# Moving the last score weights, the fold of q and the gate's small steps in a linear-attention and product-key kernel

## Chip, cores and metric

The kernel runs on one core of a Trainium2 chip. The metric is the device time of one launch in microseconds (us): the median of several runs. The profile is one further execution, taken by the hardware profiler. The engines are named as the profile names them: PE (TensorE; PEld is its weight load), DVE (VectorE), ACT (ScalarE), POOL (GpSimd) and SP (SyncE, which here only issues transfers).

## The reference, cut to what matters

One input x of 2048 rows and 512 columns goes through two branches, and a gate mixes them.

```python
g = sigmoid((x * gate_w).sum(-1, keepdims=True))
# branch A: linear attention, 32 heads of 16, feature map learned per head
q, k, v = x @ wqkv                       # split into heads
phi_q = concat(softmax(q @ w_phi), softmax(-(q @ w_phi)))
phi_k = concat(softmax(k @ w_phi), softmax(-(k @ w_phi)))
kv = sum_s phi_k[s]^T v[s];  z = sum_s phi_k[s]
a = (phi_q @ kv) / (phi_q @ z + 1e-6) @ wo
# branch B: product keys, 32 heads, 16 x 16 = 256 experts, the best one per head
s1 = (x @ w_q)[..., :128] @ k1.T;  s2 = (x @ w_q)[..., 128:] @ k2.T
e = 16 * argmax(s1) + argmax(s2)         # one expert per row and head
b = sum_h gelu(x . u[e_h]) * v[e_h]      # softmax over one score is 1
out = g * a + (1 - g) * b
```

## The kernel before

The 2048 rows are 16 tiles (`NT`) of 128. All large products are done in three passes on a value split into a rounded high half and the remaining low half (`xh`, `xl` and so on): high by high, high by low, low by high (`mm3`, lines 54 to 56). `split` makes the halves: ACT copies the high half, DVE subtracts.

The schedule is written by hand: each engine runs its instructions in the order in which the program issues them, and each waits for its data. So a waiting instruction holds everything behind it on its engine, and SP's transfers are in order too.

**First loop, t = 0 to 15 (line 283 on): the sums over k and the weights.** For each tile `vproj` and `kproj` project v and k on PE; `softmax_diffs` makes the differences for both softmaxes on DVE (lines 90, 92, 94, 96); ACT takes the exponential (L315); `ksoft` sums and inverts on DVE (L179, L180) and multiplies on POOL (L181); `kvacc` adds phi_k^T v on PE (L188). The last two tiles' sums are made after the loop, and `kvz` (L196) adds their z part with a column of ones.

Between these, the loop builds what the second loop needs. w_phi is folded into the weights of k and q (`fold`, PE L147, high halves ACT L137, low halves DVE L138; one pair of tiles, `wah` and `wal`, holds first k's and then q's folded weights). The product-key scores use w_q folded with the keys: for each of eight blocks j, `score_w` (L204) makes two products, `score_planes` copies the result as two 16-bit planes (ACT L209) and has the DMA transpose them (SP L211), and `score_join` puts the planes together (ACT L216), copies the high half into `sh` (ACT L220) and subtracts the low half into `sl` (POOL L221). The plane tile `wpl`, the transposed tile `wtp` and the joined tile `wtj` have one buffer each. `joins` holds blocks transposed but not joined; at the start of a tile's middle part they move to `old` and are joined at that tile's end, and in tile 15 ahead of its exponential. `plan` places the last products: block 6 is complete in tile 12, block 7 in tile 14. In tile 14, `eh` and `el`, the halves of the expert values, are split as well. In tile 15 PE folds q in two halves, with the two halves of the first tile's scores (`front_s`, s = x by `sh`/`sl`) behind them, and the fold is evicted after `ksoft`.

**Between the loops:** `kvz`, the best keys of tile 0 (`best`), the projection of q with the folded weights (`front_q`, tile pq), the gate and expert products (`front_p`, tile pp), the copy `zc` of the sums z, and `z_final`, which spreads z over all partitions on PE (L619).

**Second loop, a = 0 to 14, and a tail written out for the last tiles.** It is a software pipeline over three tiles: scores, q and gate of the next tile (n and a), the counting of chosen experts of tile b = a - 1 (`count`, a chain of some twenty small DVE steps that `step` deals out between others), and the output product of z = a - 2. `gelu_pre` and `gate` make the sigmoid of the gate from `exp(-p)`: `gs[:,0]` is the exponential, `gs[:,1]` adds one, `gs[:,2]` inverts, `gs[:,3]` is half of one minus the gate. `gelu_act` then applies the tanh and that factor. `coef` (L558) multiplies the counts by the activated values; it runs on POOL up to tile 13 and on DVE for 14 and 15.

Of the kernel before, what the change touches and what calls it, by code (L numbers as in the profile page):

```python
# [15 lines left out]
AF = mybir.ActivationFunctionType  # L16
ALU = mybir.AluOpType
# [6 lines left out]
NT = S // P  # L24
# [9 lines left out]
def mix_kernel(ctx, tc, xT, wqT, wkT, wv, wphi, wo, wq, kk, ug, ev, cst, out):  # L34
# [98 lines left out]
    def fold(raw, wh, wl, n_, halves=True):  # L133
        def evict(g):
            for q in range(4):
                part = o[q].rearrange("p (g c) -> p g c", c=32)[:, g]
                act.copy(fv(wh, q)[:, g], part)  # L137
                dve.tensor_tensor(fv(wl, q)[:, g], part, fv(wh, q)[:, g], op=ALU.subtract)  # L138

        o = [tr_bank(f"fold{n_}{q}") if q < 3 else mm_bank(f"fold{n_}{q}") for q in range(4)]  # L140
        for i in range(2):
            for k in (2 * i, 2 * i + 1):
                for b in range(NK):
                    for q in range(4):
                        r = slice(32 * q, 32 * q + 32)
                        c0 = (k * NK + b) * 32
                        pe.matmul(o[q][:, c0:c0 + 32], raw[r, b, k * P:(k + 1) * P], wp[r, b, :],  # L147
                                  start=True, stop=True, skip_group_check=True)
            yield
            if halves:  # L150
                evict(slice(8 * i, 8 * i + 8))
                yield
        if not halves:
            evict(slice(0, 16))
            yield
# [27 lines left out]
    def kvacc(t):  # L183
        n = F + 1 if t < NT - 2 else F
        for g in range(8):
            for c in range(4):
                h = 4 * g + c
                pe.matmul(acc[32 * c:32 * c + 32, g, :n], phis[t][:, 32 * h:32 * h + 32],  # L188
                          vs[t][:, h, :n], start=(t == 0 and g == 0),
                          stop=(t == NT - 1), skip_group_check=True)  # L190
# [23 lines left out]
    def score_join(j, tp):  # L214
        tj = wa_.tile([P, D], F32, tag="wtj", bufs=1, name=f"wtj{j}")
        act.copy(tj.bitcast(U16).rearrange("p (k n j) -> p j k n", j=2, n=P),  # L216
                 tp.rearrange("p (j k) n -> p j k n", j=2))
        js = slice(P * j, P * j + P)
        t3 = tj.rearrange("p (k e) -> p k e", k=NK)
        act.copy(sh[:, :, js], t3)  # L220
        pool.tensor_tensor(sl[:, :, js], t3, sh[:, :, js], op=ALU.subtract)  # L221
# [3 lines left out]
    def front_s(t, half):  # L225
        e = st8[t]
        e[half] = mm_bank(f"s{half}_{t}")
        proj(e[half], t, sh, sl, 512 * half, 512 * half + 512)
# [55 lines left out]
    for t in range(NT):  # L284
        if t + 3 < NT:
            x_load(t + 3)
        if 2 < t < NT - 2:
            vproj(t)()
        kproj(t)
        old = list(joins)  # L290
        joins.clear()
        for _ in range(plan.get(t, 0)):
            score_w(done, raws[done])
            done += 1
            if done + 1 < 16:
                raws.append(stage(wq[done + 1], f"wq{done + 1}"))
            elif done == 15:
                rawq = stage(wqT, "rawq")
            if done % 2 == 0:
                score_planes(done // 2 - 1)  # L300
        if t == 11:
            rawu = [spare(ug[:, 0:2], "rawu0", [P, 2, NU])]
        if t == 12:
            rawu.append(spare(ug[:, 2:4], "rawu1", [P, 2, NU]))
        if t == 13:
            rawe = [spare(ev[:, 0], "rawe0", [P, D])]
        if t % 2 == 0:
            for u in (t - 3, t - 2):
                if u >= 0:
                    kvacc(u)  # L310
        if t == NT - 1:
            for j, tp in old:
                score_join(j, tp)
            old = []
        act.activation(phis[t], phis[t], AF.Exp)  # L315
        if 0 < t < NT - 2:
            x_split(t + 2)
        if t == 13:
            for k in range(NK):
                split(uh[:, k, :], ul[:, k, :], rawu[k // 2][:, k % 2, :])  # L320
            rawe.append(spare(ev[:, 1], "rawe1", [P, D]))
        if t == 14:
            for k in range(2):
                split(eh[:, k, :], el[:, k, :], rawe[k])
        if t == NT - 1:
            fq = fold(rawq, wah, wal, "q", False)
            next(fq)
            front_s(0, 0)
            next(fq)
            front_s(0, 1)  # L330
            kvacc(NT - 3)
        ksoft(t)
        if t == NT - 1:
            next(fq)
        for j, tp in old:
            score_join(j, tp)
    ca.close()
# [19 lines left out]
    def gelu_pre(t):  # L357
        pp = st8[t]["pp"]
        gs = w2.tile([P, 4], F32, name=f"gs{t}", tag="gs")
        act.activation(gs[:, 0:1], pp[:, NX:NX + 1], AF.Exp, scale=-1.0)  # L360
        px = w2.tile([P, NX], F32, name=f"px{t}", tag="px")
        x2 = w2.tile([P, NX], F32, name=f"x2{t}", tag="x2")
        act.copy(px, pp[:, :NX])
        act.activation(x2, pp[:, :NX], AF.Square)
        act.activation(x2, x2, AF.Copy, bias=GELU_C, scale=0.044715 * GELU_C)
        st8[t].update(g=gs, G=px, x2=x2)

    def gate(t):
        gs = st8[t]["g"]
        yield dve.tensor_scalar_add(gs[:, 1:2], gs[:, 0:1], 1.0)  # L370
        yield dve.reciprocal(gs[:, 2:3], gs[:, 1:2])
        yield dve.tensor_scalar(gs[:, 3:4], gs[:, 2:3], -0.5, 0.5, op0=ALU.mult, op1=ALU.add)

    def gelu_in(t):
        px, x2 = st8[t]["G"], st8[t]["x2"]
# [1 line left out]

    def gelu_act(t):
        x2, gs = st8[t]["x2"], st8[t]["g"]
        act.activation(x2, x2, AF.Tanh)  # L380
        act.activation(x2, x2, AF.Identity, bias=gs[:, 3:4], scale=gs[:, 3:4])

# [9 lines left out]
    def soft_in(t, step=lambda: None):  # L392
        e = st8[t]
        d = w2.tile([P, 1024], F32, tag="d", name=f"d2{t}")
        st = w2.tile([P, 320], F32, tag="stt", name=f"st2{t}")
        softmax_diffs(e["pq"], d, st, step)
        e.update(ph=d, st=st)
# [157 lines left out]

    def coef(t):
        e = st8[t]
        (pool if t < NT - 2 else dve).tensor_tensor(e["C"], e["C"], e["G"], op=ALU.mult)  # L558

    def back_c(t):  # L560
        e = st8[t]
# [72 lines left out]
    turn_eq(0)  # L634
    front_q(0)
    soft_in(0)
    kvz(NT - 1)
    act.copy(zc, acc[:, :, F])
    front_p(0)
    z_final()  # L640
    wo_load((0, 1))
    for a in range(NT - 1):
        n, b, z = a + 1, a - 1, a - 2
        B, Z = b >= 0, z >= 0
        if Z:
            mid_num(z)
            back_c(z)
        if B:
            planes(b)
            front_q(a)  # L650
        if a == 1:
            v14, v15 = vproj(NT - 2), vproj(NT - 1)
        gelu_in(a)
        if Z:
            num_lo(z)
            back_cl(z)
        for _ in gate(a):
            step(b)
        gelu_act(a)
        if B:  # L660
            step(b, 2)
            soft_in(a, lambda: step(b, 2))
            drain(b)
        if a == 1:
            v14()
        soft_exp(a)
        if a == 1:
            v15()
            for k in range(2):
                act.copy(wbh[:, k, :], rawo[k])  # L670
        if Z:
            back_o(z)
            back_ol(z)
            back_out(z)
            store(z)
        mid_mask(a)
        front_s(n, 0)
        if a == 1:
            kvacc(NT - 2)
            kvacc(NT - 1)  # L680
            cl_.close()
            w4 = ctx.enter_context(tc_pool("w4", "right"))
        front_s(n, 1)
        front_p(n, False)
        soft_w(a)
        soft_sum(a, 0)
        soft_sum(a, 1)
        if a == 1:
            for k in range(2):
                pool.tensor_tensor(wbl[:, k, :], rawo[k], wbh[:, k, :], op=ALU.subtract)  # L690
            wo_load((2, 3))
        best(n, 0)
        soft_y(a, 0)
        soft_y(a, 1)
        if B:
            join(b)
            gelu_out(b)
            coef(b)
        if a == 1:
            kv_final()  # L700
            for k in range(2, NK):
                act.copy(wbh[:, k, :], rawo[k])
        soft_b(a)
        if a == 1:
            for k in range(2, NK):
                pool.tensor_tensor(wbl[:, k, :], rawo[k], wbh[:, k, :], op=ALU.subtract)
        best(n, 1)
        turn_eq(n)
        gelu_pre(n)
# [9 lines left out]
    for _ in gate(a):  # L719
        step(b)  # L720
    gelu_act(a)
    step(b, 2)
    soft_in(a, lambda: step(b, 2))
    drain(b)
    coef(b)
# [85 lines left out]
```

## Time and profile before

| | us |
|---|---|
| median of 3 runs (393.65 to 393.74) | 393.67 |
| the profiled execution | 393.26 |
| its span, from the first to the last instruction | 391.5 |
| mean granted clock of PE in it | 0.991 |

A row of the timeline gives the start, the duration, the engine, the line of the kernel, the operation, what it writes and reads, the shapes and how many instructions were put together; square brackets give how long the engine sat idle before it and for whom. Matmuls are pipelined: one of 512 columns is shown as some 0.4 us long, while the next starts about 0.23 us after it. In the waits, "A <- B: total, times, longest" says that A sat idle until B was done.

### The profile page before, as it was taken

The numbers are of one execution on the slowest core, as the hardware profiler recorded it, in microseconds if no ns is written. First come the engines' busy times: TensorE is split into PE (matmuls) and PEld (weight loads), VectorE is DVE, ScalarE is ACT, GpSimd is POOL, SyncE is SP. The second block draws the span as 40 slices with busy tenths as digits, with TensorE's granted clock in tenths as the row PEclk, the third lists the DMA queues.
The fourth block names the chain that finished last, engine by engine and source line by source line (L and its number), as shares of the span: only waits on it lengthen the run. The fifth ranks groups of instructions, "written<-read, shape, count | busy, mean of one in ns | idle before, by whom it ended". The sixth has DMA issues, their size and how long they took to land.

```text
span 391.5 us, 9209 instructions
## 1 busy us (share of the span) xinstructions
PE 381.0 (97%) x3688; PEld 297.9 (76%) x3688; DVE 324.1 (83%) x831; ACT 210.3 (54%) x358; POOL 155.1 (40%) x164
## 2 busy tenths in 40 slices
PE   8999999999999899999999999999999999999975
PEld 5866787777767688877878788788788788788753
DVE  4356866766668769989999999999999999999994
ACT  4325465644645344657557556555564574574732
POOL 1004344325324332756336346345344354264340
PEclk9999999999999899999999999999999999999989
DMA  7478867478692033130650430440431331323301
GB/s 280 150 265 295 208 251 229 155 211 243 209 268 68 4 82 80 55 83 29 108 82 27 109 81 28 103 87 28 86 84 47 82 82 56 80 57 80 83 27 55
DMA packets 66715, 45.38 MB, mean 116 GB/s; under 512 B 58096, under 2 KB 58992, under 8 KB 64368
## 3 DMA queue, kind: packets, MB, share of 16 engines
q1 hardware_dynamic: 65808, 43.92, 41.4%
q10 hardware_dynamic: 864, 0.87, 0.8%
q8 instruction: 29, 0.48, 0.5%
q14 instruction: 14, 0.11, 0.1%
HBM read 26.43 MB, written 4.19 MB: 78 GB/s over the span
## 4 chain that ended last, share of the span: by engine, by line
PE 78%; DVE 13%; ACT 4%; POOL 2%; issue 2%; DMA 1%; POOLq 0%; DVEq 0%; ACTq 0%
PE s L54 6%; PE s L55 6%; PE s L56 6%; PE pv L54 4%; PE po L579 4%; PE po L585 4%; PE po L580 3%; PE pv L56 3%; PE pv L55 3%; PE pq L54 3%; PE ws L204 3%; PE pq L56 3%; PE pq L55 3%; PE pk L56 3%; PE pk L55 3%; PE pk L54 3%
## 5 line engine op out<-in xcount | busy, mean ns | idle before, releaser
L410 POOL TENSOR_TENSOR w<-d,zb 128x512 f32<-128x512 f32 x32 | 40.8, 1297 | 100.8 <-ACT d L404 100.8
L181 POOL TENSOR_TENSOR d<-d,st 128x1024 f32<-128x1024 f32 x16 | 31.0, 1939 | 77.0 <-DVE st L180 70.5
L55 PE MATMUL s<-sl,xh 128*128 128x512 f32 x128 | 50.8, 397 | 2.1 <-POOL sl L221 2.1
L54 PE MATMUL s<-sh,xh 128*128 128x512 f32 x128 | 52.4, 409 | 0.0
L56 PE MATMUL s<-sh,xl 128*128 128x512 f32 x128 | 50.8, 397 | 0.0
L404 ACT ACTIVATE d<-d 128x512 f32<-128x512 f32 x32 | 18.4, 624 | 58.8 <-DVE d L96 58.8
L440 POOL TENSOR_TENSOR d<-d,st 128x512 f32<-128x512 f32 x31 | 32.7, 1075 | 25.9 <-DVE st L434 20.8
L483 ACT COPY pt<-tp 128x1024 uint16<-128x1024 uint16 x30 | 39.0, 1371 | 1.6 <-DMA tp<-pl 0.8
L315 ACT ACTIVATE d<-d 128x1024 f32<-128x1024 f32 x16 | 17.0, 1061 | 39.0 <-DVE d L96 39.0
L473 ACT COPY pl<-d 128x1024 uint16<-128x1024 uint16 x30 | 30.5, 1060 | 2.1 <-POOL d L440 2.0
L55 PEld LDWEIGHTS s<-sl,xh 128*128 128x128 f32 x128 | 24.4, 190 | 7.0 <-POOL sl L221 2.4
L129 DVE TENSOR_TENSOR xl<-xr,xh 128x512 fp32r<-128x512 f32 (+2 forms) x17 | 11.2, 661 | 21.4 <-ACT xh L128 21.3
L56 PEld LDWEIGHTS s<-sh,xl 128*128 128x128 f32 x128 | 24.5, 191 | 5.5
L54 PEld LDWEIGHTS s<-sh,xh 128*128 128x128 f32 x128 | 24.3, 190 | 4.7
L414 DVE TENSOR_REDUCE st<-d 128x32 f32<-128x512 f32 x32 | 20.5, 681 | 8.2 <-ACT d L404 8.2
L579 PE MATMUL po<-wbh,oh 128*128 128x512 f32 x64 | 26.0, 407 | 1.1 <-ACT oh L497 1.1
L54 PE MATMUL pv<-wbh,xh 128*128 128x512 f32 x64 | 26.6, 415 | 0.6 <-ACT xh L128 0.6
L54 PE MATMUL pq<-wah,xh 128*128 128x512 f32 x64 | 26.5, 415 | 0.0
L580 PE MATMUL po<-wbl,oh 128*128 128x512 f32 x64 | 25.9, 404 | 0.0
L56 PE MATMUL pv<-wbh,xl 128*128 128x512 f32 x64 | 25.4, 396 | 0.0
L54 PE MATMUL pk<-wah,xh 128*128 128x512 f32 x64 | 25.3, 396 | 0.0
L55 PE MATMUL pv<-wbl,xh 128*128 128x512 f32 x64 | 25.3, 395 | 0.0
(147 smaller groups left out, 1026.7 us busy)
## 6 DMA issues: line engine op xcount, KB each, us to landing
wq<-wq SPq DMA_DIRECT2D x16, 1024.0 KB, 6.2
xr<-xT SPq DMA_DIRECT2D x15, 256.0 KB, 5.6
y<-ot SPq DMA_DIRECT2D x15, 256.0 KB, 2.0
rawk<-wkT SPq DMA_DIRECT2D x1, 1024.0 KB, 6.0
rawq<-wqT SPq DMA_DIRECT2D x1, 1024.0 KB, 5.2
rawo<-wo SPq DMA_DIRECT2D x4, 256.0 KB, 3.6
rawu<-ug SPq DMA_DIRECT2D x2, 258.0 KB, 6.1
rawv<-wv ACTq DMA_DIRECT2D x2, 256.0 KB, 4.5
```

The costliest lines, as they stand in the source:

```text
L54: pe.matmul(o, ah, bh, start=(first and i == 0), stop=False)
L55: pe.matmul(o, ah, bl, start=False, stop=False)
L56: pe.matmul(o, al, bh, start=False, stop=(last and i == n - 1))
L181: pool.tensor_tensor(g64(d), g64(d), b64(st[:, 128:192]), op=ALU.mult)
L404: act.activation(d[:, s_], d[:, s_], AF.Exp)
L410: pool.tensor_tensor(e["w"][:, s_], e["ph"][:, s_], zb[:, s_], op=ALU.mult)
L414: dve.tensor_reduce(e["st"][:, 64 + 32 * i:96 + 32 * i], g64(e["ph"])[:, 32 * i:32 * i + 32], axis=AX.X, op=ALU.add)
L440: eng.tensor_tensor(g64(d)[:, gs_], g64(d)[:, gs_], r[:, gs_].unsqueeze(2).to_broadcast([P, 32, F]), op=ALU.mult)
L473: act.copy(pl, e["ph"][:, s_].bitcast(U16).rearrange("p (c j) -> p j c", j=2))
L483: act.copy(p16[:, :, 4 * i:4 * i + 4, :], e["tp"][i].rearrange("p (j g) n -> p j g n", j=2))
L579: pe.matmul(po, oh[:, k, :], wbh[:, k, :], start=(k == 0), stop=False)
L580: pe.matmul(po, oh[:, k, :], wbl[:, k, :], start=False, stop=False)
```

## The change

Five things are moved. (1) The join of block 6 goes from the end of tile 13 to tile 14, ahead of its exponential, and that of block 7 from tile 15 to tile 14, behind its exponential; so it now stands ahead of the split of `eh`/`el` on ACT and of `ksoft`'s product on POOL. (2) In tile 15 the fold of q, the first scores and `kvacc` of tile 13 are issued ahead of the exponential, and the fold's eviction with them, ahead of `ksoft`. (3) Between the loops `front_p(0)` is issued ahead of the last `kvz`. (4) Two of the three small DVE steps of the gate go to ACT, into `gelu_pre` and `gelu_act`; the number of `step` calls is made up behind it. (5) `coef` of tile 14 goes from DVE to POOL.

```diff
@@ first loop
-        old = list(joins)
-        joins.clear()
+        old = [] if t == NT - 3 else list(joins)
+        if old:
+            joins.clear()
...
-        if t == NT - 1:
-            for j, tp in old:
-                score_join(j, tp)
-            old = []
+        if t == NT - 2:
+            score_join(*old.pop())
+        elif t == NT - 1:
+            fq = fold(rawq, wah, wal, "q", False)
+            next(fq)
+            front_s(0, 0)
+            next(fq)
+            front_s(0, 1)
+            kvacc(NT - 3)
+            next(fq)
         act.activation(phis[t], phis[t], AF.Exp)
+        if t == NT - 2:
+            score_join(*joins.pop())
         if 0 < t < NT - 2:
             x_split(t + 2)
...
-        if t == NT - 1:
-            fq = fold(rawq, wah, wal, "q", False)
-            next(fq)
-            front_s(0, 0)
-            next(fq)
-            front_s(0, 1)
-            kvacc(NT - 3)
         ksoft(t)
-        if t == NT - 1:
-            next(fq)
         for j, tp in old:
             score_join(j, tp)
@@ gelu_pre, gate, gelu_act
         act.activation(gs[:, 0:1], pp[:, NX:NX + 1], AF.Exp, scale=-1.0)
+        act.activation(gs[:, 1:2], gs[:, 0:1], AF.Copy, bias=1.0)
...
-        yield dve.tensor_scalar_add(gs[:, 1:2], gs[:, 0:1], 1.0)
         yield dve.reciprocal(gs[:, 2:3], gs[:, 1:2])
-        yield dve.tensor_scalar(gs[:, 3:4], gs[:, 2:3], -0.5, 0.5, op0=ALU.mult, op1=ALU.add)
...
+        act.activation(gs[:, 3:4], gs[:, 2:3], AF.Copy, scale=-0.5, bias=0.5)
         act.activation(x2, x2, AF.Tanh)
@@ coef
-        (pool if t < NT - 2 else dve).tensor_tensor(e["C"], e["C"], e["G"], op=ALU.mult)
+        (pool if t < NT - 1 else dve).tensor_tensor(e["C"], e["C"], e["G"], op=ALU.mult)
@@ between the loops
     soft_in(0)
+    front_p(0, False)
     kvz(NT - 1)
     act.copy(zc, acc[:, :, F])
-    front_p(0)
+    gelu_pre(0)
@@ second loop and tail, behind gelu_act(a)
-            step(b, 2)
+            step(b, 4)
             soft_in(a, lambda: step(b, 2))
```

More of the change, by code (lines that the diff above doesn't have):

```diff
@@ L721, in mix_kernel @@
     gelu_act(a)
-    step(b, 2)
+    step(b, 4)
     soft_in(a, lambda: step(b, 2))
```

## The prediction

> **What bounds the kernel now.** I read the page first, then who waited for whom on TensorE, then the busy time in stretches of 3.41 us, and last the timeline from 114 to 140 us and at the end. A row of the stretches gives the stretch, its length, PE's busy time with the count of matmuls, and the granted clock.
>
> ```profile
> span 391.5 us, 9209 instructions
> PE 381.0 (97%) x3688; PEld 297.9 (76%) x3688; DVE 324.1 (83%) x831; ACT 210.3 (54%) x358; POOL 155.1 (40%) x164
> ```
> ```profile
> PE s L55 <- POOL sl L221: 2.1, 1, 2.1
> ```
> ```profile
> 126.39:129.81 3.42, 1.33 (x10) 1.00 0.00 0
> 129.81:133.22 3.41, 3.41 (x9) 0.50 0.02 5
> 372.15:375.57 3.42, 1.48 (x14) 1.00 0.12 49
> 375.57:378.98 3.41, 3.41 (x10) 0.50 0.07 28
> 385.80:389.21 3.41, 2.18 (x10) 1.00 0.00 0
> ```
>
> TensorE (PE) sets the time: it is busy for 97% of the span, and only one wait between the start and the last tile is longer than a microsecond. That wait, for the low half of the last score weights (sl, written by POOL at L221), lies where the first loop hands over to the second. It costs more than its 2.1 us. The stretch that contains it has PE busy for 1.33 of 3.42 us, and in the next 3.41 us the granted clock is 0.50: half of 3.41, another 1.7 us, is lost. The same follows a stretch with 1.48 busy near the end; 2.18 busy is followed by nothing in this table. So the removable loss at the handover is 3.8 us, if nothing new waits there.
>
> **The change, part by part: the score weights.** These rows are the timeline of before at the handover.
>
> ```profile
> 116.02 1.36 ACT L216 COPY wtj<-wtp 128x1024 uint16<-128x1024 uint16 x1
> 117.41 0.62 ACT L220 CAST sh<-wtj 128x512 fp32r<-128x512 f32 x1
> 117.94 1.01 ACT L209 COPY wpl<-ws 128x1024 uint16<-128x1024 uint16 x1
> 118.97 1.25 SPq L211 DMA_TRANSPOSE wtp<-wpl  x1
> 122.00 1.12 ACT L48 CAST eh<-rawe 128x512 fp32r<-128x512 f32 x2
> 122.63 1.29 DVE L49 TENSOR_TENSOR el<-rawe,eh 128x512 fp32r<-128x512 f32 x2 [1.63 <-ACT eh L48]
> 123.84 1.21 DVE L179 TENSOR_REDUCE st<-d 128x64 f32<-128x1024 f32 x1
> 123.94 1.35 ACT L216 COPY wtj<-wtp 128x1024 uint16<-128x1024 uint16 x1 [0.83 <-DMA wtp<-wpl]
> 125.09 0.55 DVE L180 RECIPROCAL st<-st 128x64 f32<-128x64 f32 x1
> 125.81 1.93 POOL L181 TENSOR_TENSOR d<-d,st 128x1024 f32<-128x1024 f32 x1 [3.80 <-DVE st L180]
> 127.29 0.68 DVE L96 TENSOR_TENSOR d<-st,pk 128x512 f32<-128x512 f32 x1
> 127.70 1.27 POOL L221 TENSOR_TENSOR sl<-wtj,sh 128x512 fp32r<-128x512 f32 x1
> 129.02 0.50 PE L55 MATMUL s<-sl,xh 128*128 128x512 f32 x1 [2.09 <-POOL sl L221]
> 130.87 2.42 DVE L138 TENSOR_TENSOR wal<-foldq,wah 128x512 fp32r<-128x512 f32 x4
> ```
>
> Join 6 (the first L216 and L220) now follows the plane copy of join 7 (L209) instead of preceding it, so that copy starts at 116.02, not 117.94. The transpose does not start 1.9 us earlier, though: its target wtp has one buffer, which join 6 must first have read. At tile 4 of before the order was already the new one:
>
> ```profile
> 51.51 1.36 ACT L216 COPY wtj<-wtp 128x1024 uint16<-128x1024 uint16 x1
> 52.90 1.24 SPq L211 DMA_TRANSPOSE wtp<-wpl  x1
> ```
> ```profile
> DMA to landing us min/median/max: 3.1/3.1/3.1
> DMA to landing us min/median/max: 4.9/4.9/4.9
> ```
>
> The transpose there left as the copy out of wtp ended. Here join 6's copy would run from about 116.95 to 118.3, so the transpose leaves at 118.35, 0.6 us earlier than at 118.97. Nothing else stands in SP's queue behind it until the first tile's mask. How long it flies is the first unknown. The two landing times are that of the transpose at 52.90 (3.1 us) and that of the one at 118.97 (4.9 us). At 3.1 it would land at 121.5, and join 7 would start when ScalarE is free, at 122.0 (where L48 starts now); at 4.9 at 123.3; if something else than the issue holds its last part, at 123.9 as today. I take 122.3, near the short flight, because SP issues nothing between the loads of ev, which are well ahead of it, and this transpose. Call this start L; today it is 123.94.
>
> From L the rows give: two ScalarE steps of join 7 take 1.92 (116.02 to 117.94), then POOL's sl is 1.3 long and no longer stands behind the 1.93 of L181. It ends at L + 3.4 = 125.7. PE ran dry for it at 126.9 (129.02 less 2.09), so that wait is gone for any L up to 123.5.
>
> The price: the split of eh now stands behind join 7 on ScalarE, and DVE's el, in order, stands before the sums, the reciprocal and the four softmax differences of the last tile. DVE waits at el instead of working. From L: 1.92 to the start of eh, 0.63 to el (122.00 to 122.63), 1.21 to the sums, 1.25 to the reciprocal, 2.88 to the end of the differences (125.09 to 127.29 + 0.68). They end at L + 7.9 = 130.2 where before they ended at 127.97.
>
> **Fold of q and the reordered start.** In program order PE comes next to the sums kvacc and kvz, then to the projection pq with the folded weights:
>
> ```profile
> 126.44 0.49 PE L54 MATMUL s<-sh,xh 128*128 128x512 f32 x1
> 133.32 0.71 PE L188 MATMUL kvacc<-v,d 128*32 128x17 f32 x62
> 134.88 0.40 PE L55 MATMUL pq<-wal,xh 128*128 128x512 f32 x1
> 137.50 0.71 PE L196 MATMUL kvacc<-ones,d 128*32 128x1 f32 x64
> 138.27 0.17 ACT L638 COPY zc<-kvacc 128x8 f32<-128x8 f32 x1 [7.22 <-PE kvacc L196]
> 139.70 0.27 PE L619 MATMUL z<-cs,zc 128*128 128x128 f32 x1
> ```
>
> Eleven matmuls at full clock take 2.62 us (134.88 to 137.50). So the twelve of the second score half, begun at 126.44, end near 129.3; kvacc ends at 129.9, and kvz of tile 14 needs POOL's product, which now starts at L + 5.7 = 128.0 and ends at 130.0: no wait worth counting. PE reaches pq at 130.6 and can do one matmul; the second needs wal. The four wal subtractions no longer wait for the last exponential, sums and reciprocal, but they start after the differences and take 2.42: wal is complete at L + 10.2 = 132.5. This is a new wait of 1.7 us (130.9 to 132.6), in place of the 2.09. Still the second pq matmul runs at 132.6 instead of 134.88, 2.3 us earlier, because the old wait and the half clock lay before it.
>
> From there to z there was 4.82 us of work (134.88 to 139.70). It is the same work in another order, pp now before the last kvz. That hides the later last k sums (DVE 132.5 to 134.3, POOL to 136.3, kvz not before 136.8), but the copy zc, which pp used to cover, stands open: 0.17 and its two hand-overs, 0.55 in my estimate (bounds 0.3 and 0.8). So z starts at 132.6 + 4.8 + 0.55 = 138.0 instead of 139.70: 1.7 us gained, which PE, never idle in the tiles that follow, carries to the last tile.
>
> **Whether the clock drops again** is the second unknown. In a stretch placed as above, 129.81 to 133.22, PE would be busy for 3.41 - 1.72 = 1.7 us. Drops follow 1.33 and 1.48, none is seen after 2.18; 1.7 lies between, nearer to the drops. A drop would cost up to 1.7. I take no drop, as the new wait is shorter than the one before by 0.4 and a landing at the 122.0 bound shortens it by another 0.3.
>
> The Trainium skill, TensorE: Matmul & The Clock Gate, section "Why this matters for your kernels", says that only gaps of more than about 3 us between bursts bring the clock down. By that rule no drop would follow here and the time would be my forecast; the trace does not agree, since 2.09 us of waiting was enough.
>
> **Gate and coef.** Two tiny DVE steps per tile go to ScalarE.
>
> ```profile
> DVE mx L448 <- PE s L56: 1.2, 6, 0.2
> ```
> ```profile
> 332.89 0.17 ACT L360 ACTIVATE gs<-pp 128x1 f32<-128x1 f32 x1 [2.16 <-PE pp L56]
> 333.97 0.63 ACT L497 CAST oh<-oT 128x256 fp32r<-128x256 f32 x2
> 334.36 0.76 DVE L504 TENSOR_TENSOR ol<-oT,oh 128x256 fp32r<-128x256 f32 x2
> ```
>
> The added step depends on the one just before it, so ScalarE's next steps move by about 0.2. The cast oh is one of them, and DVE's ol follows its first half by less than 0.1 (333.97 + 0.31 to 334.36): DVE is moved by 0.2 too. What it saves later is little, since the small steps fill the gaps between dependent ones. DVE has 0.2 of waiting for PE per tile to absorb this (six waits, 1.2 in all). I count zero in the loop; bounds: a gain of 0 and a loss of 0.1 per tile over 13 tiles, 1.3. In the last tile nothing absorbs it.
>
> ```profile
> L558 POOL TENSOR_TENSOR cf<-cf,px x14: 727/736/742, 164.5 to 361.0; 128x256 f32<-128x256 f32 x14
> ```
> ```profile
> 373.07 0.42 DVE L558 TENSOR_TENSOR cf<-cf,px 128x256 f32<-128x256 f32 x1
> 373.37 2.52 POOL L410 TENSOR_TENSOR w<-d,zb 128x512 f32<-128x512 f32 x2 [6.50 <-ACT d L404]
> 375.59 1.27 DVE L418 TENSOR_REDUCE st<-w 128x32 f32<-128x512 f32 x2
> ```
>
> There coef of tile 14 goes from DVE (0.42) to POOL (0.74), ahead of the product w. Moved by 0.2, coef ends on POOL at 374.0, w at 376.5 instead of 375.9, and the second sum over w, 0.68 long, at 377.2 instead of 376.86. The rest of the end hangs on it: a loss of 0.3 (bounds 0 and 0.6).
>
> **Sum.** 1.7 gained, 0.3 lost: 1.4 less. The profiled execution took 393.26 us, 391.5 of them its span; the median of the runs is 393.67. The difference applied to the median gives 392.3.
>
> **The rivals.** *The drop comes again.* For: 1.7 busy is nearer to 1.48 than to 2.18. Against: the new wait is shorter than any that was followed by a drop. z would start at 139.7 as before, and with the end's 0.3 the time is 393.9 (393.3 to 394.8). Chance 0.26.
>
> *Slower: the transpose lands as late as today, and DVE is held behind el.* L = 123.94 puts wal at 134.15, kvz of tile 14 waits for POOL until 131.6, and PE idles 1.7 and then 1.7 us around it. The drop is then certain by the table, and 2.4 us of pq and pp run at half clock, a loss of 1.2: z at 139.6 + 1.2 = 140.8, 1.1 later than before, with the end 395.1. It decides from L = 123.7 even without a drop, and from L = 122.0 with one. For: the last landing took 4.9. Against: the transpose leaves earlier and nothing new is put ahead of it. Chance 0.22.
>
> *The gate on ScalarE makes DVE the bound.* If the 0.2 of slack is not there in most tiles, 1.3 of the gain goes: 393.6. For: DVE's slack per tile is as small as the shift. Against: ScalarE's start is tied to PE, so a DVE that falls behind no longer waits for oh. Chance 0.06.
>
> **How the numbers follow.** A measurement of this kernel can tell about 0.2%, 0.8 us, from no change. The forecast has chance 0.46, with its own range of 391.4 to 392.9 (end 0 to 0.6, zc 0.3 to 0.8, L from 122.0 to 122.8), nearly all faster. The drop is mostly within 0.8 us (0.20) and else slower (0.06); the late landing is slower (0.20) or same (0.02); the gate is same (0.05) or slower (0.01). That makes faster 0.45, same 0.28, slower 0.27. The range 391.4 to 395.0 leaves out the worse half of the late landing and little below.
>
> **What would show it.** Right: PE's wait for sl gone; a wait of PE at L55 of pq for wal of about 1.7 us; DVE waiting at el until about 124.9; z's first matmul near 138.0; one stretch of half clock fewer. Step by step wrong: the transpose not waiting for join 6; L far from 122.3; a 0.50 stretch after the pq wait (then 393.9); the second sum over w not later by 0.3; DVE's waits for PE at L448 gone and PE waiting in the loop. A gain of over 3 us would say that DVE did not stand still at el.

## The result: no measurable change, from two groups of runs

| | us |
|---|---|
| before, median of 20 runs (393.32 to 394.85) | 393.82 |
| changed, median of 20 runs (392.64 to 395.59) | 394.28 |
| ratio of the means, changed to before, 95% interval | 1.0001 [0.9989, 1.0012] |
| changed, profiled execution: time, span | 394.27, 392.5 |

The 20 runs of the changed kernel are not spread evenly. Six lie between 392.64 and 393.11, thirteen between 394.14 and 394.57, one at 395.59, and nothing between 393.11 and 394.14. The lower and the upper group are 1.7 us apart, which is half of a 3.4 us stretch at half clock. All 20 runs of before lie in one band. The forecast (392.3, own range 391.4 to 392.9) describes the lower group, whose median of 392.78 is 0.5 above it; the rival "the drop comes again" (393.9, 393.3 to 394.8) describes the upper one, and the upper one is the larger. The profiled execution belongs to it.

The mean granted clock of the runs agrees, as far as it goes: it is 0.996 in all six lower runs, 0.991 or less in eleven of the other fourteen, and 0.996 in three. It counts one more stretch of half clock, the one near the end that the prediction's table shows, and that one costs nothing that the times show: in the run e10 below, an execution with a mean clock of 0.996 and one with 1.000 both took 392.71. So a run with half clock at the handover and none near the end would have 0.996 as well.

The page, the waits of PE and the stretches of the changed kernel:

```profile
span 392.5 us, 9192 instructions
PE 381.1 (97%) x3688; PEld 297.2 (76%) x3688; DVE 322.3 (82%) x798; ACT 214.7 (55%) x390; POOL 156.0 (40%) x165
```
```profile
PE pq L55 <- DVE wal L138: 1.5, 1, 1.5
PE kvacc L196 <- POOL d L181: 0.3, 1, 0.3
```
```profile
130.91:134.32 3.41, 1.87 (x68) 1.00 0.02 5
134.32:137.74 3.42, 3.42 (x9) 0.50 0.00 0
137.74:141.15 3.41, 3.13 (x84) 1.00 0.56 105
```

The wait for sl (2.1 us) is gone and a wait for wal (1.5 us) has come, with 0.3 ahead of it for the product of tile 14. The stretch that holds both is followed by 3.42 us at a granted clock of 0.50, as in before. PE's busy time is the same to 0.1 us: one stall has been traded for another.

The timeline of the changed kernel at the handover:

```profile
117.46 1.35 ACT L216 COPY wtj<-wtp 128x1024 uint16<-128x1024 uint16 x1
118.84 1.25 SPq L211 DMA_TRANSPOSE wtp<-wpl  x1
122.58 1.36 ACT L216 COPY wtj<-wtp 128x1024 uint16<-128x1024 uint16 x1
124.66 1.27 POOL L221 TENSOR_TENSOR sl<-wtj,sh 128x512 fp32r<-128x512 f32 x1 [2.12 <-ACT sh L220]
125.14 1.96 DVE L49 TENSOR_TENSOR el<-rawe,eh 128x512 fp32r<-128x512 f32 x2 [3.60 <-ACT eh L48]
126.98 0.50 PE L54 MATMUL s<-sh,xh 128*128 128x512 f32 x1
131.05 2.48 DVE L138 TENSOR_TENSOR wal<-foldq,wah 128x512 fp32r<-128x512 f32 x4
133.58 0.50 PE L55 MATMUL pq<-wal,xh 128*128 128x512 f32 x1 [1.48 <-DVE wal L138]
140.31 2.05 PE L619 MATMUL z<-cs,zc 128*128 128x128 f32 x16 [0.28 <-ACT zc L639]
```

This execution runs 0.54 us late from well before the change (the second score half starts at 126.98, before at 126.44). With that taken off, the transpose leaves at 118.30, join 7 starts at 122.04, sl ends at 125.39, el starts at 124.60, wal ends at 132.99, pq goes on at 133.04 and z starts at 139.77. The end is then 252.2 us behind z's start (392.5 - 140.31), in before 251.8.

### The profile page after: what moved, and what is told of

It reads as the page before. It is cut to its first block, busy times and chain, and to the rows that moved or that the text cites. A ratio compares the mean times of both kernels' runs of the same rounds, so it can differ in the third digit from the quotient of the medians.

```text
span 392.5 us, 9192 instructions
## 1 busy us (share of the span) xinstructions
PE 381.1 (97%) x3688; PEld 297.2 (76%) x3688; DVE 322.3 (82%) x798; ACT 214.7 (55%) x390; POOL 156.0 (40%) x165
## 4 chain that ended last, share of the span: by engine, by line
PE 77%; DVE 11%; ACT 4%; POOL 2%; DMA 2%; issue 2%; ACTq 0%; POOLq 0%
PE s L54 6%; PE s L56 6%; PE s L55 6%; PE pv L54 4%; PE po L585 4%; PE po L579 4%; PE po L580 3%; PE ws L204 3%; PE pv L56 3%; PE pv L55 3%; PE pq L55 3%; PE pq L56 3%; PE pq L54 3%; PE pk L54 3%; PE pk L56 3%; PE pk L55 3%
## 5 line engine op out<-in xcount | busy, mean ns | idle before, releaser
L55 PE MATMUL s<-sl,xh 128*128 128x512 f32 x128 | 50.0, 390 | 0.0
L55 PE MATMUL pq<-wal,xh 128*128 128x512 f32 x64 | 25.8, 403 | 1.5 <-DVE wal L138 1.5
L56 PE MATMUL pq<-wah,xl 128*128 128x512 f32 x64 | 25.7, 402 | 0.0
```

Of the source, the lines that this page charges most:

```text
L55: pe.matmul(o, ah, bl, start=False, stop=False)
L56: pe.matmul(o, al, bh, start=False, stop=(last and i == n - 1))
```

## The experiments

**Late split of eh (e1).** Is the wait for wal made by DVE, held in order behind el?

```diff
-        if t == 14:
-            for k in range(2):
-                split(eh[:, k, :], el[:, k, :], rawe[k])
...
             next(fq)          # tile 15: the fold's eviction
+            for k in range(2):
+                split(eh[:, k, :], el[:, k, :], rawe[k])
```

> The changed kernel with the split of eh and el issued behind the fold's eviction in tile 15 instead of behind the join of block 7 in tile 14. Theory (DVE is held in order behind el, and that makes the wait for wal): the last tile's differences end near 127.5 instead of 131.1, the 1.5 us wait at pq's L55 is gone or under 0.3 us, no half clock at the handover in any run, z starts some 3.5 us earlier; time 390.6 us (390.0 to 391.2), all runs in one group. Rival (the landing of the transpose or DVE's own load sets wal): a wait of over 1 us at L55 stays, time 392.5 to 394.6 in two groups as now.

Measured: 390.7 (390.57 to 390.75), ratio to before 0.9906 [0.989, 0.9921]; all five runs in one group. The timeline:

```profile
127.54 2.48 DVE L138 TENSOR_TENSOR wal<-foldq,wah 128x512 fp32r<-128x512 f32 x4 [0.89 <-ACT wah L137]
129.94 1.28 DVE L49 TENSOR_TENSOR el<-rawe,eh 128x512 fp32r<-128x512 f32 x2
136.37 2.05 PE L618 MATMUL z<-cs,zc 128*128 128x128 f32 x16 [0.28 <-ACT zc L638]
138.75 0.36 PE L511 MATMUL mk<-wm,et 128*128 128x16 bf16 x8 [0.33 <-DMA et<-eq]
```

wal starts 3.5 us earlier than in the changed kernel, PE's list of waits no longer has pq, and z starts 3.9 us earlier (0.15 of both is this execution's own: its second score half starts at 126.83, there at 126.98). The position of one split decides. It is also a version that beats both kernels: 3.3 us under the 394.0 of the runs of before that were taken beside it. Some 0.3 us of the gain is given back at once, since the first mask now waits for its transpose.

**Six filler matmuls in the wait (e2).** Does the half clock follow PE's idle time?

```diff
         pq = mm_bank(f"pq{t}")
+        if t == 0:
+            for _ in range(6):
+                pe.matmul(pq, xh[:, 0, 0, :], sh[:, 0, 0:512], start=True, stop=True)
         proj(pq, t, wah, wal, 0, D)
```

> The changed kernel with six matmuls of 512 columns (their result is overwritten) put on TensorE between kvz of tile 14 and the projection pq of tile 0, that is into the 1.5 us wait for wal: 1.4 us of work that nothing waits for. Theory (the half clock follows TensorE's idle time): no 0.50 stretch at the handover in any run, so the runs form one group at the level of the faster group of the changed kernel, 392.8 us (392.5 to 393.3). Rival (the drop comes from elsewhere, such as where the execution starts): two groups 1.7 us apart stay, most runs at 394.3.

Measured: 392.72 (392.54 to 393.22, six runs), ratio 0.9959 [0.9945, 0.9974]. The upper group is gone, with nothing done but useless work in the wait. The stretches of this kernel at the same place, and z:

```profile
130.91:134.32 3.41, 3.32 (x75) 1.00 0.02 5
134.32:137.74 3.42, 3.42 (x38) 1.00 0.00 0
```
```profile
138.58 2.05 PE L622 MATMUL z<-cs,zc 128*128 128x128 f32 x16 [0.28 <-ACT zc L642]
```

So what separates the two groups is the clock, and the change without the drop is worth 1.3 us (392.72 against 394.0 for the runs of before beside it).

**Three fillers (e10).** How much idle time is enough?

```diff
-            for _ in range(6):
+            for _ in range(3):
```

> The changed kernel with three matmuls of 512 columns in the wait for wal instead of the six of the run e2: 0.7 us of the 1.5 us wait is filled, some 0.8 us stay idle. The wait costs the same to the work that follows, so only the clock can differ. Theory (the half clock depends on how much of a 3.4 us stretch is idle, and 1.1 us of idle with the wait before it is under the limit): one group at 392.7 us (392.4 to 393.3) as with six. Rival (any wait of near a microsecond brings the drop in some runs): some runs at 394.3.

Measured: 392.7, 392.71, 392.71, 392.74 and 394.22. The rival was right: one run in five still has the drop, and it is the profiled one.

```profile
130.30:133.71 3.41, 2.32 (x87) 1.00 0.02 5
133.71:137.12 3.41, 3.41 (x9) 0.50 0.00 0
```

Here 2.32 us of busy time were followed by half clock, while 2.18 in the prediction's table were not. PE's busy time alone is therefore not the measure. The kind of work may count: 64 of the 87 matmuls here have a single column (kvz, 0.65 us of the 2.32), and only five have 512; the 2.18 were eight or nine of 512. A stretch early in the run e6 (below) points the same way. PE is busy in all of it, 64 of its 70 matmuls are the small ones of the fold of k, and half clock follows:

```profile
15.84:19.25 3.41, 3.41 (x70) 1.00 0.00 0
19.25:22.66 3.41, 3.41 (x10) 0.50 0.81 295
```

But counting the wide matmuls is not the rule either. In e3 and e4 (below) two stretches are nearly alike: each has the 64 narrow matmuls of kvacc and the 64 of kvz, and two or three of 512 columns start in it. The one of e3 (first two rows) is followed by half clock, the one of e4 (last two rows) by full clock:

```profile
129.61:133.02 3.41, 2.23 (x131) 1.00 0.02 5
133.02:136.44 3.42, 2.83 (x7) 0.50 0.00 0
```
```profile
129.13:132.54 3.41, 2.31 (x133) 1.00 0.00 0
132.54:135.95 3.41, 0.49 (x1) 1.00 0.02 5
```

So how much idle time is enough stays open: no run here isolates it.

**Fillers in the kernel before (e9).** The same for the old wait for sl, with nothing of the change in it.

```diff
-            front_s(0, 1)
+            s1 = mm_bank("s1_0")
+            for _ in range(9):
+                pe.matmul(s1, xh[:, 0, 0, :], sh[:, 0, 0:512], start=True, stop=True)
+            proj(s1, 0, sh, sl, 512, 1024); st8[0][1] = s1
```

> The kernel before with nine matmuls of 512 columns (their result is overwritten) ahead of the second half of tile 0's scores, that is into its 2.1 us wait for sl: 2.05 us of work that nothing waits for. Theory (half of what the wait costs is the half clock behind it): the wait shrinks to under 0.3 us with z starting 1.7 us earlier and no half clock at the handover: 392.1 us (391.8 to 392.5), beside the changed kernel's faster group though nothing of the change is in it. Rival (the wait alone costs): 393.9 as before.

Measured: 392.54 (392.1 to 393.67, six runs) against 394.23 for the runs of before beside it, ratio 0.9962 [0.9948, 0.9976]. The slowest of the six, at 393.67, has a mean clock of 0.991, as runs with the drop have; the others took at most 392.61.

```profile
126.40:129.80 3.40, 3.34 (x28) 1.00 0.00 0
```

PE goes on with the scores no sooner than before, and the 1.7 us come from the clock alone. The old stall did cost these 1.7 us on top of its waiting.

**The joins alone (e4).** The kernel before with the first three hunks' moves of the joins, and the fold evicted where it was.

```diff
-        old = list(joins)
-        joins.clear()
+        old = [] if t == NT - 3 else list(joins)
+        if old:
+            joins.clear()
...
-        if t == NT - 1:
-            for j, tp in old:
-                score_join(j, tp)
-            old = []
+        if t == NT - 2:
+            score_join(*old.pop())
         act.activation(phis[t], phis[t], AF.Exp)
+        if t == NT - 2:
+            score_join(*joins.pop())
```

> The kernel before with the joins of blocks 6 and 7 moved as in the change, and nothing else. Theory (el holds DVE, and without the early eviction wal comes behind the last exponential, sums and reciprocal): the wait for sl is gone, the wait for wal is 3.5 to 4.5 us, half clock after it in every run, time 395.6 us (394.6 to 396.6), slower than before. Rival (moving the joins is itself the gain and the fold's move adds little): 392 to 393.5.

Measured: 397.02 (396.71 to 399.3), ratio 1.0066 [1.0049, 1.0083]: slower, as the theory says, and by 1.4 us more than it said.

```profile
PE pq L54 <- ACT wah L137: 2.6, 1, 2.6
PE pq L55 <- DVE wal L138: 1.7, 1, 1.7
```
```profile
132.54:135.95 3.41, 0.49 (x1) 1.00 0.02 5
135.95:139.36 3.41, 2.78 (x7) 0.50 0.00 0
139.36:142.78 3.42, 3.42 (x71) 0.50 0.62 102
142.78:146.19 3.41, 3.41 (x17) 0.50 0.41 131
```

The wait is 4.3 us, as expected (3.5 to 4.5). The half clock behind it lasts three stretches instead of one: 10.2 us. The first begins with idle time; the second is full, but 64 of its 71 matmuls are the single columns of the last kvz. Full clock returns behind the third, the first of them that is full and without kvz. Why the first did not end it is open, for the half-clock stretch of e3 above, with 2.83 us busy, did. The profiled execution is also the slowest of the seven (399.3, mean clock 0.983; the others 0.987 to 0.991), so the others had less half clock than this.

**The fold and pp alone (e8).** The kernel before with the early eviction, and pp ahead of the last kvz.

```diff
         if t == NT - 1:
             for j, tp in old:
                 score_join(j, tp)
             old = []
+            fq = fold(rawq, wah, wal, "q", False)
+            next(fq); front_s(0, 0); next(fq); front_s(0, 1)
+            kvacc(NT - 3)
+            next(fq)
...
+    front_p(0, False)
     kvz(NT - 1)
     act.copy(zc, acc[:, :, F])
-    front_p(0)
+    gelu_pre(0)
```

> The kernel before with the early eviction of the fold and the first tile's pp ahead of the last kvz, and the joins, the gate and coef as before. Theory (the wait for sl and its half clock stay; wal is early but nothing waited for it; the copy zc stands open for some 0.5 us): 0.3 to 0.6 us slower than before, 394.3 against 393.9. Rival (the early eviction is a gain by itself): faster than 393.3.

Measured: 394.41 (393.76 to 395.89) against 394.23, ratio 1.0012 [0.9999, 1.0025]: 0.2 us by the medians, less than expected, and the interval just reaches no change. The 12 runs form two groups. Five, at 395.16 to 395.89, have a mean clock of 0.987, that is one stretch of half clock more; the other seven have 0.991, and their median is 394.0, no more than before's. The trace has the old wait unchanged, and z at 139.85 with the copy zc open ahead of it:

```profile
PE s L55 <- POOL sl L221: 2.1, 1, 2.1
```
```profile
139.85 2.05 PE L617 MATMUL z<-cs,zc 128*128 128x128 f32 x16 [0.28 <-ACT zc L637]
```

So neither half of the first-loop change is worth anything alone: the joins alone lose 3 us, and the eviction with pp gains nothing.

**Gate and coef.** Both back on DVE in the changed kernel (e3), each of them in the kernel of e1 (e5, e6), and both there (e7).

```diff
-        act.activation(gs[:, 1:2], gs[:, 0:1], AF.Copy, bias=1.0)
+        yield dve.tensor_scalar_add(gs[:, 1:2], gs[:, 0:1], 1.0)
...
-    (pool if t < NT - 1 else dve).tensor_tensor(e["C"], e["C"], e["G"], op=ALU.mult)
+    (pool if t < NT - 2 else dve).tensor_tensor(e["C"], e["C"], e["G"], op=ALU.mult)
```

> The changed kernel with the gate's three small steps back on DVE and coef of tile 14 back on DVE. Theory (coef on POOL delays the last product w, the gate's steps are neutral): the loop is the same within 0.1 us per tile, the second sum over w ends 0.2 to 0.4 us earlier after the last exponential, and both groups of runs lie 0.3 us lower: 392.5 and 394.0. Rival (the gate on ScalarE relieves DVE): 0.2 to 1 us slower than the changed kernel in each group.

> The kernel of the run e1 (the change, with the split of eh late; 390.7 us) with the gate's three small steps back on DVE; coef of tile 14 stays on POOL. Theory (the gate's steps are neutral: what ScalarE adds ahead of oh, DVE saves in the count chain): 390.7 us within 0.15. Rival from the prediction (the gate on ScalarE delays DVE in the last tile): 0.2 to 0.3 us faster, 390.45. Rival of the other side (it relieves DVE): 0.3 us or more slower.

> The kernel of the run e1 with coef of tile 14 back on DVE; the gate stays on ScalarE. Theory (coef on POOL stands ahead of the last w and delays the end): 0.2 to 0.4 us faster, 390.4. Rival (DVE is the later one at the end, so that coef on POOL gains): 0.2 us or more slower.

> The kernel of the run e1 with the gate's steps and coef of tile 14 both back on DVE, that is only the moves of the joins, of the fold and of pp, with the split of eh late. Theory (gate neutral, coef on POOL costs 0.2): 390.5 us in runs without another spell of half clock, from the last exponential to the end of the second sum over w 4.2 us as before. Rival (the gate or coef gain): 390.9 us or more and 4.4 us.

Measured: e3 394.08 (392.64 to 394.45, 12 runs, three of them in a lower group again); e5 391.09 (390.52 to 392.47); e6 391.09 (390.32 to 391.95); e7 390.69 (390.46 to 390.75), ratio to before 0.9907 [0.9894, 0.9921], beside e1's 0.9906. In the profiles of e5 and e6 the clock was lower elsewhere too (0.95 in place of 1.00 in e5's, and in e6's the stretch at 0.50 that starts 19 us into it), and the runs of both spread over 1.6 us and more, so their times decide nothing; e3's groups differ from the changed kernel's by less than their width. The traces decide. The last exponential, coef, w and the second sum, of the changed kernel and then of e3:

```profile
373.48 1.15 ACT L404 ACTIVATE d<-d 128x512 f32<-128x512 f32 x2 [0.80 <-DVE d L96]
373.95 0.72 POOL L558 TENSOR_TENSOR cf<-cf,px 128x256 f32<-128x256 f32 x1 [6.26 <-DVE cf L554]
374.63 2.52 POOL L410 TENSOR_TENSOR w<-d,zb 128x512 f32<-128x512 f32 x2
376.40 1.47 DVE L418 TENSOR_REDUCE st<-w 128x32 f32<-128x512 f32 x2
```
```profile
373.39 1.15 ACT L404 ACTIVATE d<-d 128x512 f32<-128x512 f32 x2 [0.93 <-DVE d L96]
374.10 2.51 POOL L410 TENSOR_TENSOR w<-d,zb 128x512 f32<-128x512 f32 x2 [6.49 <-ACT d L404]
376.32 1.27 DVE L418 TENSOR_REDUCE st<-w 128x32 f32<-128x512 f32 x2
```

From the exponential to the end of the second sum it is 4.39 us with coef on POOL and 4.20 without; in e1 and e5, which have it on POOL, 4.41 and 4.40, in e6 and e7, which do not, 4.21. coef on POOL costs 0.2 us there. For the gate, the rows from the sigmoid's exponential to the first softmax step of the last tile, before and then changed:

```profile
363.19 0.17 ACT L360 ACTIVATE gs<-pp 128x1 f32<-128x1 f32 x1 [2.16 <-PE pp L56]
364.65 0.76 DVE L504 TENSOR_TENSOR ol<-oT,oh 128x256 fp32r<-128x256 f32 x2
368.57 0.68 DVE L90 TENSOR_REDUCE st<-pq 128x32 f32<-128x512 f32 x1
```
```profile
364.00 0.17 ACT L360 ACTIVATE gs<-pp 128x1 f32<-128x1 f32 x1 [2.16 <-PE pp L56]
365.70 0.76 DVE L504 TENSOR_TENSOR ol<-oT,oh 128x256 fp32r<-128x256 f32 x2
369.38 0.68 DVE L90 TENSOR_REDUCE st<-pq 128x32 f32<-128x512 f32 x1
```

ol comes 1.46 us behind the exponential before and 1.70 in the changed kernel, but the softmax step 5.38 behind it in both. What ScalarE adds, DVE saves a few steps later. The loop shows no difference either: from z's first matmul to the last exponential it is 233.2 us in the changed kernel and in e3 (its z starts at 140.20). The gate is neutral.

## Why the prediction was right, and where it was not

The measured time lies inside the range only because the range took in the rivals. The likeliest case was the wrong one: the forecast of a gain came true in 6 of 20 runs, and the median is that of the first rival. The lower group is 1.0 us under before (392.78 against 393.82) where 1.4 was forecast.

- **The transpose waits for join 6:** right. It left at 118.84 as join 6's copy ended (117.46 + 1.35), 1.3 us later than the plane copy, which ended at 117.56, would have allowed. It did not matter: it flew 3.1 us, ScalarE was the later one, and join 7 began with no wait listed, at 122.04 in before's time, the lower bound given (122.0; I took 122.3). The short flight was right, its reason was not shown. In before fifteen of the transpose's sixteen parts had landed by 122.34 and the last at 123.87, and a transfer of 16 KB of instructions ran from 121.84 to 122.77; whether that held the last part, and why nothing held one here, was not tried.
- **The wait for sl goes:** right.
- **DVE is held behind el:** right, shown by e1. One term was mis-sized: el took 1.96 us, not 1.29. Its first half ran beside POOL's sl (124.66 to 125.93) and took 1.35; in e1, where POOL was idle, each half took 0.68 and both together 1.28. The Trainium skill, SBUF — State Buffer, section "Who interferes with whom", says that a DVE operation with two SBUF inputs and a POOL operation that reads SBUF share one read port and block each other; the rows agree. With L 0.3 early and el 0.67 late, wal ended at 133.0 instead of 132.5.
- **A new wait of 1.7 us for wal:** 1.48, and 0.3 for kvz of tile 14, which I had put at none. That the sum is right is luck: PE came to pq later and wal was complete later, both by some 0.5 us.
- **No drop of the clock:** this step failed. I compared busy times, 1.7 between 1.48 and 2.18, and took no drop because the wait was shorter than the old one. The stretch was 1.87 us busy, with four matmuls of 512 columns, as before's had, and the 64 of kvz, 0.6 us; half clock followed. It also followed 2.23 us in e3 and 2.32 in e10, so a busy time of 1.7 gave no ground for full clock, and being shorter than one other wait gave none. What decides is open, as the rows under e10 show, and so is which runs escape. What differs between executions is where the 3.4 us stretches fall: the first spell of full clock begins 6.93 us into the profile of before and 4.62 us into that of the changed kernel, and every later change of the clock lies a whole number of stretches behind it. No run tried that. The old wait let a run escape too, though rarely: one of the 17 runs of before beside e1 took 392.26, with a mean clock of 0.996.
- **zc open, 0.55:** the step is there, but was mis-sized. PE waits 0.28 for it, under the lower bound of 0.3, and from the second pq matmul to z it is 5.04 us in e8 (134.81 to 139.85) against 4.82 before: 0.2 in all. This made up for part of wal's delay: in e2, without the drop, z starts at 138.2 in before's time (138.58, with the second score half at 126.84), near the 138.0 forecast.
- **Gate:** I had it delay the last tile by 0.2; that falls, it is neutral. **coef:** 0.2, as one part of the 0.3 put on the end. The changed kernel's way from z to the end is 0.4 longer; the other 0.2 arises before the last exponential and is in e3 too (392.2 - 140.20 = 252.0), where gate and coef are as before. e8 has it as well (392.0 - 139.85 = 252.15). Both have pp's new place and the early eviction; what makes it was not tried.
- **The slower rival** (a late landing) did not occur; e4 shows its mechanism with another cause.

## What to carry to other kernels

When a wait on the bounding engine is removed, look at the next operand that this engine needs and at what was pushed back to free the first: here two ScalarE casts, not needed before the second loop's third tile, were left in a place where an in-order DVE had to wait for them, and moving them turned no change into a gain of 3.3 us. A stall of 1.5 to 2 us on PE cost another 1.7 us here where the clock dropped behind it, and filling it with useless wide matmuls is a cheap test of how much of the cost is the clock.

## What the runs showed of the hardware

The granted clock fell to 0.50 behind stretches with 1.33, 1.48, 1.87, 2.23 and even 2.32 us of PE busy in 3.41, and once behind a full one whose matmuls were mostly small (e6). It did not fall behind 2.18 us of 512-column matmuls, nor behind 2.31 us of mostly narrow ones (e4). It did not fall in the same way in every execution (by their times in 14 of 20 runs of the changed kernel, in 1 of 5 in e10). In before and in the changed kernel it lasted one stretch; in the profile of e4, behind a wait of 4.3 us and with single-column matmuls in what followed, it lasted three (10.2 us). The first half of el, beside a POOL subtraction on SBUF, took 1.35 us instead of 0.68.
